# Another order of loads and other slots for the K and V tiles of a cached attention block

## The chip, the cores and the metric

The kernel runs on one core of one Trainium2 chip. The metric is the device time of one execution in microseconds. A core has five engines with an instruction list each: TensorE (PE: matmuls, PEld: its weight loads), VectorE (DVE), ScalarE (ACT), GpSimd (POOL) and SyncE (SP), which here only issues loads and stores. Each engine works through its list in order; engines wait for each other on semaphores. Sixteen DMA engines, shared by all loads, move data from the chip's memory (HBM) into the on-chip memory (SBUF).

## The reference, cut to what matters

One decode step: two batch rows `x` of 512 numbers go through a layer norm, an attention over a cache of 32768 keys and values in 8 key/value heads (32 query heads, 128 numbers each), and a gated two-layer network whose result scales the attention's output. All is float32.

```python
xn = layernorm(x)                                   # x: (2, 1, 512)
q = (xn @ wq) -> (2, 32, 1, 128)                    # 4 query heads share one K/V head
scores = einsum("bhqd,bhkd->bhqk", q, k) * 128**-0.5   # k, v: (2, 8, 32768, 128)
s = einsum("bhqk,bhkd->bhqd", softmax(scores), v) -> (2, 1, 4096) @ wo
gate = xn @ W_gate; up = xn @ W_up
g = silu(((gate * (gate > 0)) * up) @ W_down)
out = x + s * g
```

The caches are 2 x 268 MB, read once; everything else is small.

## The kernel before

The 16 pairs of batch row and K/V head are the **groups** (`NG` = 16, index `g`). A group's K and its V are two tiles each, K0, K1, V0, V1, of 16384 keys: 128 partitions x 16384 numbers, 8 MB. Such a tile fills one of three large SBUF slots. The weights `wq` (a full slot), `W_gate` with `W_up` (a slot together), `W_down` and, at the end, `wo` use the same slots.

What is done in a group (`attend`): VectorE transposes K0 in place in blocks of 32 (`turn`, L487, one instruction) and K1 in two halves; TensorE forms the scores of both (`score`, 32 matmuls a tile, into the PSUM tile `s`). Then comes the softmax: VectorE takes the maximum (L509), a chain of short TensorE and VectorE steps makes the bias, ScalarE the exponentials (L532), TensorE permutes them (`pts`), VectorE transposes them into `pt` (L542) and makes the reciprocal of the sum (L555). TensorE multiplies them with V0 and V1 (`values`, 32 matmuls a tile, into `o_ps`), and `gather` scales the result (L578) and folds it into `stage` (L599).

Ahead of the groups stands the **head**: the query projection from `wq`, whose result goes to `qz`; the products with `W_gate` and `W_up` (PSUM tile `pts`), three VectorE steps on them (L448, L452, L454), and the product with `W_down` (PSUM tile `m_ps`). Behind them stands the **tail**: `gather_all` puts the heads together (`ot_ps`, `ot`), and the product with `wo`, in six pieces (16, 8, 4, 2, 1 and 1 of its 32 rows a partition), ends in `res` and four small stores.

What sets the order. `Program.add` writes down, for each operation, which tiles it reads and writes, and derives its waits from that. Each engine's list is the order in which `add` is called; nothing reorders it. All loads but that of `x` are issued by SP, so they too are one list: a load that waits for its slot holds up all loads behind it. Slots go round: load number n goes to slot n mod 3, and `freed(n)`, called behind the last use of load n, issues load n + 3. The order of the tiles is K0, K1, V0, V1 of a group, then the next group. TensorE's list for the first 15 groups is a hardware loop of 5 trips with three groups as its body (`emit_loop`), since after three groups (12 tiles) the slots repeat; the other engines' lists are written out.

GpSimd clears and fills small constant tiles at the start (L246 to L281, L329) and copies the queries of each group into one of three buffers `qg` (L612).

Of the kernel before, what the change touches and what calls it, by code (L numbers as in the profile page):

```python
# [3 lines left out]
F32 = mybir.dt.float32  # L4
# [6 lines left out]
Q = 32  # L11
# [119 lines left out]
def decode_block(nc, x, kc, vc, wq, wo, wg, wu, wd, out):  # L131
# [19 lines left out]
    def sb(name, *shape):  # L151
        return nc.alloc_sbuf_tensor(name, list(shape), F32).ap()

    ring = [nc.alloc_sbuf_tensor(f"r{k}", [P, SLOT], F32, align_bytes=512).ap() for k in range(SLOTS)]
# [4 lines left out]
    qz = sb("qz", P, NG, 4, CR)  # L159
    qg = [sb(f"qg{k}", P, CR + P) for k in range(SLOTS)]  # L160
    place = sb("place", P, 3 + CR + 1)
    eye = sb("eye", P, 2 * P - CR)
    same = sb("same", P, Q, REP)
# [23 lines left out]
    def G(emit, reads=(), writes=()):  # L187
        pr.add("pool", emit, reads, writes)
# [19 lines left out]

    def freed(n):
        n += SLOTS  # L210
        g, i = divmod(n - SLOTS, 4)
        dst, names = slot(n)
        if g == NG and i == 0:
            worows = wo.rearrange("(p i) d -> p (i d)", p=P)
            row = 0
            for k, m in enumerate(WO_PIECES):
                span = slice(row * D, (row + m) * D)
                load(dst[:, span], worows[:, span], f"wo{k}", [("wo", k)] + (names if k == 0 else []))
                row += m
        elif g < NG:  # L220
            rows, kind = rows_of((kc, vc)[i // 2], g, i % 2), "kkvv"[i] + str(i % 2)
            if g == NG - 1 and i == 3:
                m = SLOT // 2
                for s in range(NS):
                    part = slice(s * m, (s + 1) * m)
                    load(dst[:, part], rows[:, part], kind + "b" * s, names[s : s + 1])
            else:
                load(dst, rows, kind, names)


    wqs, gus, wds = ring[:3]
    load(wqs[:, : NKC * QN], wq.rearrange("(p i) n -> p (i n)", p=P), "wq", slot(0)[1])
    for n, (src, kind) in enumerate(((wg, "wg"), (wu, "wu"))):
        load(
            gus[:, n * NKC * F : (n + 1) * NKC * F],
            src.rearrange("(p i) f -> p (i f)", p=P),
            kind,
            [(1, n)],
        )
    load(wds[:, : FI * D], wd.rearrange("(p i) d -> p (i d)", p=P), "wd", slot(2)[1])  # L240
    xp, xc = pt[:32, 0], pt[:32, 1]
# [83 lines left out]
    )  # L325
    n = 1
    while n < Q:
        G(
            lambda n=n: pool.tensor_copy(same[:, n : 2 * n, :], same[:, :n, :]),  # L329
            ["same"],  # L330
            ["same"],
        )
        n *= 2
    V(
# [42 lines left out]
        ),  # L377
        ["xnp"] + slot(0)[1],
        ["S"],
    )  # L380
    freed(0)
    V(lambda: dve.tensor_copy(w, S), ["S"], ["w"])  # L382
# [45 lines left out]
    for n in range(2):  # L428
        T(
            lambda n=n: matmuls(  # L430
                (
                    pts[32 * c : 32 * c + 32, n, :FC],
                    xnp[:, i, :],
                    gut[:, n, i, c * FC : (c + 1) * FC],
                    i == 0,
                    i == NKC - 1,
                )
                for i in range(NKC)
                for c in range(4)
            ),  # L440
            ["xnp", (1, n)],
            ["pts"],
        )
    freed(1)
    gate = w[:, 0, :FC]
# [11 lines left out]
    )  # L457
    T(
        lambda: matmuls(
            (  # L460
                m_ps[32 * (i % 4) : 32 * (i % 4) + 32, :],
                ht[:, i, :],
                wdt[:, i, :],
                i < 4,
                i >= FI - 4,
            )
            for i in range(FI)
        ),
        ["pt0"] + slot(2)[1],
        ["m"],  # L470
    )
    freed(2)
    part_d = os.rearrange("p c d -> p (c d)")
    V(lambda: dve.tensor_copy(part_d, m_ps), ["m"], OS)
    T(
        lambda: matmuls(
            (ot_ps[32 * c : 32 * c + 32, :P], fold, part_d[:, c * P : (c + 1) * P], True, True)
            for c in range(4)
        ),
        ["fold"] + OS,  # L480
        ["ot_ps"],
    )
    A(lambda: act.activation(gy, ot_ps[:, :P], AF.Silu), ["ot_ps"], ["gy"])


    def turn(tile, names, part):
        V(lambda: dve.transpose(tile[:, part], tile[:, part]), names, names)  # L487

    def score(g, u, s, tile, names):
        mov = tile.rearrange("p (s c j e k) -> p s c e j k", s=NS, c=NC, j=NJ, e=4)  # L490
# [12 lines left out]
            ),  # L503
            [f"qg{g % SLOTS}", names[s]],
            ["S"],
        )

    def softmax(g):
        V(lambda: dve.tensor_reduce(mx, S, axis=AX.XY, op=ALU.max), ["S"], ["mx"])  # L509
        T(lambda: pe.transpose(m_ps[:1, :P], mx, ident), ["mx", "ident"], ["m"])  # L510
        V(
            lambda: dve.tensor_reduce(  # L512
# [43 lines left out]

    def values(g, u, ss, tile, names):
        v = tile.rearrange("p (s c j d) -> p s j c d", s=NS, c=NC, j=NJ)
# [15 lines left out]

    def gather(g):
        b, hk = g % B, g // B
        V(
# [31 lines left out]
    def queries(g):  # L609
        k = g % SLOTS  # L610
        to = qg[k][:, CR:].rearrange("p (e q) -> p e q", e=4)[:, :, :CR]
        G(lambda: pool.tensor_copy(to, qz[:, g]), QZ, [f"qg{k}"])  # L612

    whole, half = slice(0, SLOT), SLOT // 2

    def attend(g):
        last = g == NG - 1
        queries(g)
        first = SLOTS + 4 * g
        k0, k1, v0, v1 = (slot(first + i) for i in range(4))  # L620
        turn(*k0, whole)
        for s in range(NS):
            turn(k1[0], k1[1][s : s + 1], slice(s * half, (s + 1) * half))
        for u, k in enumerate((k0, k1)):
            for s in range(NS):
                score(g, u, s, *k)
            freed(first + u)
        softmax(g)
        values(g, 0, range(NS), *v0)
        freed(first + 2)  # L630
        if last:
            for s in range(NS):
                values(g, 1, [s], *v1)
        else:
            values(g, 1, range(NS), *v1)
        freed(first + 3)
        gather(g)

    pr.add("pe", None, ["same", "place", "ident", "negs", "pt1"] + PERM, ["S", "pts", "m", "r", "o"])
    start = len(pr.ops["pe"])  # L640
    for g in range(NG):
        attend(g)
        if g == NG - 2:
            end = len(pr.ops["pe"])


    def gather_all(hks):
        return matmuls(
            (
                ot_ps[:, : B * Q],  # L650
                eye[:CR, P - CR - CR * hk : 2 * P - CR - CR * hk],
                stage[:CR, hk].rearrange("p b i -> p (b i)"),
                hk == 0,
                hk == HKV - 1,
            )
            for hk in hks
        )
# [10 lines left out]
    )  # L668
    wos, _ = slot(SLOTS + 4 * NG)
# [5 lines left out]
    py, pw = S[:, 0], S[:, 1]  # L675
    V(lambda: dve.memset(pw, 0.0), writes=["S", "pw"])  # L676
    bounds = [sum(WO_PIECES[:k]) for k in range(len(WO_PIECES) + 1)]
# [98 lines left out]
```

## Time and profile before

| | |
|---|---|
| time, median of 3 runs (lowest, highest) | 1314.77 us (1313.4, 1315.34) |
| the profiled execution: its time, its span | 1313.29 us, 1311.4 us |
| PE busy | 665.6 us (51%), 4680 matmuls |
| DVE busy | 632.2 us (48%), 204 instructions |
| ACT, POOL busy | 23.7 us (2%), 8.7 us (1%) |
| mean granted TensorE clock | 0.748 of full speed |
| read from HBM | 564.66 MB, 431 GB/s over the span |

The span runs from the first to the last instruction of the profiled execution, and its times count from the span's start. A row of the timeline gives start, duration, engine, line and operation, then in brackets how long the engine had been idle and what released it; "x64" counts merged instructions, and a float32 matmul of the program appears as two passes. L202 is the line of a helper that issues nearly all matmuls, so matmuls are told apart by their tiles: `s<-r,qg` are scores, `o_ps<-r,pt` are values.

### The profile page before, as it was taken

Reading aid. Unit: us, or ns where it says so; the run is one execution under the profiler, and the core shown is the slowest. Engines: PE = TensorE matmul, PEld = TensorE weight load, DVE = VectorE, ACT = ScalarE, POOL = GpSimd, SP = SyncE. Lnnn points to the kernel's source line nnn. Section 1 sums busy time; section 2 is a strip of 40 time slices with the busy share of each in tenths; the row PEclk is TensorE's granted clock in tenths of the full one; section 3 lists DMA queues with packets and bytes.
Section 4 is the critical chain, followed back from the end, with each engine's and each line's share of the span. In section 5 each row is a group of like instructions: output and inputs, shape, how many; then the busy total and the mean of one; then the engine's idle time right before and its main releaser. Section 6 shows DMA issues by size and latency. Waiting matters only on the chain.

```text
span 1311.4 us, 9865 instructions
## 1 busy us (share of the span) xinstructions
PE 665.6 (51%) x4680; PEld 186.2 (14%) x4680; DVE 632.2 (48%) x204; ACT 23.7 (2%) x37; POOL 8.7 (1%) x43
## 2 busy tenths in 40 slices
PE   3536164472616538262563726356372645637268
PEld 0202011120101102010110201011020111201012
DVE  1183562817356191744719165370925527183560
ACT  0000000000000000000000000000000000000000
POOL 1000000000000000000000000000000000000000
PEclk9768687785868777586776758778676877867688
DMA  9999999999999999999999999999999999999997
GB/s 409 438 444 422 440 424 436 428 434 442 432 434 434 432 432 434 442 434 432 434 432 436 436 438 434 430 434 434 442 428 438 434 430 434 432 444 430 436 424 331
DMA packets 10834, 564.88 MB, mean 431 GB/s; under 512 B 1210, under 2 KB 1218, under 8 KB 1604
## 3 DMA queue, kind: packets, MB, share of 16 engines
q1 hardware_dynamic: 10808, 564.67, 99.5%
q8 instruction: 11, 0.18, 0.0%
q14 instruction: 3, 0.02, 0.0%
q10 hardware_dynamic: 12, 0.01, 0.0%
HBM read 564.66 MB, written 0.00 MB: 431 GB/s over the span
## 4 chain that ended last, share of the span: by engine, by line
DMA 47%; DVE 26%; PE 25%; ACT 1%; issue 1%; DVEq 0%
DMA r<-in_A_k_cache_dram 45%; DVE r L487 21%; PE o_ps L202 11%; PE s L202 8%; PE pts L202 5%; DMA r<-in_A_wq_dram 2%; DVE pt L542 2%; DVE mx L509 2%; ACT w L532 1%; PE m_ps L202 1%; DVE mr L512 0%; PE m_ps L510 0%; DVE mrow L519 0%; DVE nb L530 0%; PE ot_ps L202 0%
## 5 line engine op out<-in xcount | busy, mean ns | idle before, releaser
L487 DVE STREAM_TRANSPOSE r<-r 128x8192 f32<-128x8192 f32 (+1 forms) x48 | 552.8, 11542 | 171.1 <-DMA r<-in_A_k_cache_dram 171.1
L202 PE MATMUL s<-r,qg 128*32 128x512 f32 x2048 | 296.4, 737 | 523.3 <-DVE r L487 523.3
L202 PE MATMUL o_ps<-r,pt 128*16 128x512 f32 x2048 | 247.6, 645 | 18.8 <-DVE rl L555 18.0
L202 PEld LDWEIGHTS s<-r,qg 128*32 128x32 f32 x2048 | 71.0, 132 | 738.1 <-DVE r L487 556.8
L578 DVE SCALAR_TENSOR_TENSOR os<-o_ps,rl,mask 128x512 f32<-128x512 f32 x16 | 12.0, 751 | 251.2 <-PE o_ps L202 251.2
L202 PEld LDWEIGHTS o_ps<-r,pt 128*16 128x16 f32 x2048 | 57.6, 103 | 195.5 <-issue 173.4
L509 DVE TENSOR_REDUCE mx<-s 128x1 f32<-128x1024 f32 x16 | 19.6, 1225 | 92.7 <-PE s L202 92.7
L202 PE MATMUL pts<-w,perm 128*128 128x512 f32 x64 | 51.9, 958 | 23.8 <-ACT w L532 23.8
L542 DVE STREAM_TRANSPOSE pt<-pts 128x1024 f32<-128x1024 f32 x16 | 20.0, 1250 | 73.2 <-PE pts L202 73.2
L532 ACT ACTIVATE w<-s,nb 128x1024 f32<-128x1024 f32 x16 | 17.8, 1113 | 1197.3 <-DVE nb L530 1197.3
L202 PE MATMUL r_ps<-os,place 128*16 128x128 f32 x128 | 16.8, 274 | 15.6 <-DVE os L578 15.6
L202 PEld LDWEIGHTS pts<-w,perm 128*128 128x128 f32 x64 | 15.0, 258 | 37.4 <-ACT w L532 25.2
L202 PEld LDWEIGHTS r_ps<-os,place 128*16 128x16 f32 x128 | 11.1, 96 | 31.5 <-DVE os L578 30.3
L510 PE MATMUL m_ps<-ident,mx 128*1 128x128 f32 x16 | 4.3, 270 | 21.7 <-DVE mx L509 21.7
L202 PE MATMUL s<-r,xnp 128*32 128x512 f32 x64 | 8.7, 706 | 9.1 <-DMA r<-in_A_wq_dram 9.1
L599 DVE TENSOR_REDUCE stage<-r_ps 16x32 f32<-16x128 f32 x16 | 4.5, 278 | 18.2 <-PE r_ps L202 18.2
L202 PEld LDWEIGHTS m_ps<-l,same 128*128 128x128 f32 x32 | 10.8, 337 | 16.0 <-issue 16.0
L202 PE MATMUL m_ps<-negs,mrow 1*128 1x1 f32 x32 | 6.6, 272 | 9.9 <-DVE mrow L519 9.9
L612 POOL COPY qg<-qz 128x64 f32<-128x64 f32 x16 | 3.7, 236 | 1019.3 <-PE s L202 996.9
L202 PE MATMUL pts<-r,xnp 128*32 128x448 f32 x64 | 8.8, 716 | 1.9 <-DVE qz L417 1.9
L202 PE MATMUL s<-r,ot 128*2 128x512 f32 (+1 forms) x88 | 8.8, 553 | 0.9 <-DVE s L676 0.9
L382 DVE COPY w<-s 128x1024 f32<-128x1024 f32 x1 | 1.2, 1225 | 16.5 <-PE s L202 16.5
(71 smaller groups left out, 77.1 us busy)
## 6 DMA issues: line engine op xcount, KB each, us to landing
r<-in_A_v_cache_dram SPq DMA_DIRECT2D x2, 4096.0 KB, 28.5
r<-in_A_wo_dram SPq DMA_DIRECT2D x1, 4096.0 KB, 26.7
r<-in_B_W_gate_dram SPq DMA_DIRECT2D x1, 3584.0 KB, 29.8
r<-in_B_W_up_dram SPq DMA_DIRECT2D x1, 3584.0 KB, 39.3
r<-in_B_W_down_dram SPq DMA_DIRECT2D x1, 3584.0 KB, 47.1
r<-in_A_wo_dram SPq DMA_DIRECT2D x1, 2048.0 KB, 31.2
r<-in_A_wo_dram SPq DMA_DIRECT2D x1, 1024.0 KB, 33.1
r<-in_A_k_cache_dram SPq DMA_DIRECT2D x32, 35.5
```

Of the source, the lines that this page charges most:

```text
L202: ins = pe.matmul(out_, lhs, rhs, start=start, stop=stop)
L382: V(lambda: dve.tensor_copy(w, S), ["S"], ["w"])
L487: V(lambda: dve.transpose(tile[:, part], tile[:, part]), names, names)
L509: V(lambda: dve.tensor_reduce(mx, S, axis=AX.XY, op=ALU.max), ["S"], ["mx"])
L510: T(lambda: pe.transpose(m_ps[:1, :P], mx, ident), ["mx", "ident"], ["m"])
L532: lambda: act.activation(w, S, AF.Exp, bias=nb, scale=SCALE, accum_out=l),
L542: lambda: dve.transpose(pt.rearrange("p u n -> p (u n)"), pts.rearrange("p u n -> p (u n)")),
L578: lambda: dve.scalar_tensor_tensor(os, o_ps, rl, mask.unsqueeze(2).to_broadcast([P, NC, DH]), op0=ALU.mult, op1=ALU.mult,),
L599: lambda: dve.tensor_reduce(stage[:CR, hk, b], r_ps[:CR, :P].rearrange("p (c i) -> p i c", c=NC), axis=AX.X, op=ALU.add,),
L612: G(lambda: pool.tensor_copy(to, qz[:, g]), QZ, [f"qg{k}"])
```

## The change

The three slots get fixed tenants: `SB` the K0 tiles, `SA` the K1 tiles, `SC` the V0 and V1 tiles in turn. K runs one group ahead: while a group's values are formed, the K tiles of the next group are loaded and scored. The order of loads is therefore K, V, K, V: V1 of g, K0 of g + 2, V0 of g + 1, K1 of g + 2. `wq` stands in `SA`, `W_gate` with `W_up` and then `W_down` in `SC`, and K0 of group 0 is loaded as the second tile, into `SB`. A trip of `attend(g)` is now: scores of K0 of g + 1, values of V0 of g, scores of K1 of g + 1, values of V1 of g, softmax of g + 1 (`weights`) with the scaling and gathering of g inside it. TensorE's loop has one group as its body and 15 trips; the scores of group 0 stand ahead of the loop, the values of group 15 behind it. Most of `gather_all` (7 of 8 heads) comes ahead of the values of the last V1. The four constant tiles `qz`, `qg`, `place`, `eye` are cut from one tile `zero` that one instruction clears, `qg` is one buffer in place of three, and `same` is filled by one copy with a repeated operand in place of five.

```diff
+    SA, SB, SC = (...)                       # three slots, not a ring
+    load(wqs, wq, "wq", SA[1])
+    load_tile(SB, 0, 0, 0)                   # K0 of group 0
     W_gate, W_up -> SC
-    load(wds[:, : FI * D], wd..., "wd", slot(2)[1])
...
     query projection from SA
+    load_tile(SA, 0, 0, 1)                   # K1 of group 0
     products with W_gate, W_up
+    load(wds[:, : FI * D], wd..., "wd", SC[1])
     gate, gate * up, transpose into pt        # VectorE
+    queries(0)
+    scores(0)                                # K0 of group 0
+    load_tile(SB, 0, 1, 0)                   # K0 of group 1
     product with W_down
+    load_tile(SC, 1, 0, 0)                   # V0 of group 0
     part_d copy, fold, silu
+    scores(1)                                # K1 of group 0
+    load_tile(SA, 0, 1, 1)                   # K1 of group 1
+    queries(1)
+    maximum()
+    weights()
...
+    def scores(u):
+        tile, names = (SB, SA)[u]
+        if u == 0:
+            turn(tile, names, whole)
+        for s in range(NS):
+            if u == 1:
+                turn(tile, names[s : s + 1], slice(s * half, (s + 1) * half))
+        for s in range(NS):
+            score(u, s, tile, names)
     def attend(g):
+        ahead, last = g + 2, g == NG - 2
+        scores(0)
+        values(0, range(NS), *SC)
+        load_tile(SC, 1, g, 1)
+        if last:
+            load_tile(SB, 1, g + 1, 0)
+        else:
+            load_tile(SB, 0, ahead, 0)
+        scores(1)
+        if not last:
+            queries(ahead)
+        maximum()
+        values(1, range(NS), *SC)
+        if last:
+            load_tile(SA, 1, g + 1, 1, NS)
+        else:
+            load_tile(SC, 1, g + 1, 0)
+            load_tile(SA, 0, ahead, 1)
+        weights(g)
...
+    values(0, range(NS), *SB)
+    gather_all(range(HKV - 1))
+    for s in range(NS):
+        values(1, [s], *SA)
+    take()
+    gather(NG - 1)
+    gather_all(range(HKV - 1, HKV))
...
-    pr.emit_loop("pe", ops[start:end], (NG - 1) // SLOTS)
+    pr.emit_loop("pe", ops[start:end], NG - 1)
```

Three places show what moved. The first is the start of SP's list of loads; `r0`, `r1`, `r2` are the three slots before, `ra`, `rb`, `rc` are `SA`, `SB`, `SC`. Before:

```order
L195 DMA r0<-in_A_wq_dram 128x16384 [waits barrier_Pool_Activation_PE_DVE_SP_release]
L195 DMA r1<-in_B_W_gate_dram 128x7168
L195 DMA r1<-in_B_W_up_dram 128x7168
L195 DMA r2<-in_B_W_down_dram 128x7168
L195 DMA r0<-in_A_k_cache_dram 128x16384 [waits pe]
L195 DMA r1<-in_A_k_cache_dram 128x16384 [waits pe]
L195 DMA r2<-in_A_v_cache_dram 128x16384 [waits pe]
L195 DMA r0<-in_A_v_cache_dram 128x16384 [waits pe]
```

And now:

```order
L198 DMA ra<-in_A_wq_dram 128x16384 [waits barrier_Pool_Activation_PE_DVE_SP_release]
L198 DMA rb<-in_A_k_cache_dram 128x16384
L198 DMA rc<-in_B_W_gate_dram 128x7168
L198 DMA rc<-in_B_W_up_dram 128x7168
L198 DMA ra<-in_A_k_cache_dram 128x16384 [waits pe]
L198 DMA rc<-in_B_W_down_dram 128x7168 [waits pe]
L198 DMA rb<-in_A_k_cache_dram 128x16384 [waits pe]
L198 DMA rc<-in_A_v_cache_dram 128x16384 [waits pe]
L198 DMA ra<-in_A_k_cache_dram 128x16384 [waits pe]
L198 DMA rc<-in_A_v_cache_dram 128x16384 [waits pe]
L198 DMA rb<-in_A_k_cache_dram 128x16384
```

`W_down` is now sixth in the list, behind both K tiles of group 0, and waits for TensorE; the second load into `rb` is K0 of group 1, the first loads of V0 and V1 into `rc` follow with K1 of group 1 between them.

The second place is VectorE's list from the gate's three steps up to the first maximum. Before:

```order
L448 TENSOR_SCALAR w<-pts 128x448 [waits pe]
L452 TENSOR_TENSOR w<-w,pts 128x448 [waits dve]
L454 STREAM_TRANSPOSE pt<-w 128x448 [waits dve]
L474 COPY os<-m_ps 128x512 [waits pe]
L487 STREAM_TRANSPOSE r<-r 128x16384 [waits k0]
L487 STREAM_TRANSPOSE r<-r 128x8192 [waits k1]
```

And now:

```order
L431 TENSOR_SCALAR w<-pts 128x448 [waits pe]
L435 TENSOR_TENSOR w<-w,pts 128x448 [waits dve]
L437 STREAM_TRANSPOSE pt<-w 128x448 [waits dve]
L443 STREAM_TRANSPOSE rb<-rb 128x16384 [waits k0]
L629 COPY os<-m_ps 128x512 [waits pe]
L443 STREAM_TRANSPOSE ra<-ra 128x8192 [waits k1]
```

The transpose of K0 has moved ahead of the copy of the `W_down` product, which now stands between the transposes of K0 and K1.

The third place is TensorE's loop body as it is now, up to the softmax; the queries (`qg`) are read from the tile `zero`.

```order
L202 MATMUL s<-rb,zero 32x512 [waits pool,dve]
L202 MATMUL s<-rb,zero 32x512 x31
L202 MATMUL o_ps<-rc,pt 16x512 [waits v0]
L202 MATMUL o_ps<-rc,pt 16x512 x31
L202 MATMUL s<-ra,zero 32x512 [waits dve]
L202 MATMUL s<-ra,zero 32x512 x15
L202 MATMUL o_ps<-rc,pt 16x512 [waits v1]
L202 MATMUL o_ps<-rc,pt 16x512 x31
L468 MATMUL m_ps<-ident,mx 1x128 [waits dve]
```

Scores and values alternate, where before a group had its 64 score matmuls, its softmax, and then its 64 value matmuls; the second half of K1's scores, which reads like the first, is left out of the rows.

More of the change, by code (lines that the diff above doesn't have):

```diff
@@ L152, in sb @@
         return nc.alloc_sbuf_tensor(name, list(shape), F32).ap()
-    ring = [nc.alloc_sbuf_tensor(f"r{k}", [P, SLOT], F32, align_bytes=512).ap() for k in range(SLOTS)]
+    SA, SB, SC = (
+        (nc.alloc_sbuf_tensor(f"r{k}", [P, SLOT], F32, align_bytes=512).ap(), [(k, 0), (k, 1)])
+        for k in "abc"
+    )
     ident, xy, gy, res, perm, fold = (
@@ L158, in decode_block @@
     )
[L159 to L162, printed above, removed]
+    sizes = (NG * 4 * CR, CR + P, 3 + CR + 1, 2 * P - CR)
+    zero = sb("zero", P, sum(sizes))
+    ends = [sum(sizes[:k]) for k in range(len(sizes) + 1)]
+    qz, qg, place, eye = (zero[:, a:b] for a, b in zip(ends, ends[1:]))
+    qz = qz.rearrange("p (g e c) -> p g e c", g=NG, e=4)
     same = sb("same", P, Q, REP)
@@ L207, in rows_of, with load_tile @@
         return src[b, hk, u * TK : (u + 1) * TK, :].rearrange("(p r) d -> p (r d)", p=P)
[L209 to L232, printed above, removed]
+    def load_tile(where, kv, g, u, parts=1):
+        dst, names = where
+        rows, kind = rows_of((kc, vc)[kv], g, u), "kv"[kv] + str(u)
+        m = SLOT // parts
+        for s in range(parts):
+            part = slice(s * m, (s + 1) * m)
+            tag = f"{kind}_{s}" if parts > 1 else kind
+            load(dst[:, part], rows[:, part], tag, names if parts == 1 else names[s : s + 1])
+    wqs, gus, wds = SA[0], SC[0], SC[0]
+    load(wqs[:, : NKC * QN], wq.rearrange("(p i) n -> p (i n)", p=P), "wq", SA[1])
+    load_tile(SB, 0, 0, 0)
     for n, (src, kind) in enumerate(((wg, "wg"), (wu, "wu"))):
@@ L237, in decode_block @@
             kind,
-            [(1, n)],
+            SC[1][n : n + 1],
         )
-    load(wds[:, : FI * D], wd.rearrange("(p i) d -> p (i d)", p=P), "wd", slot(2)[1])
     xp, xc = pt[:32, 0], pt[:32, 1]
@@ L325, in decode_block @@
     )
[L326 to L333, printed above, removed]
+    G(
+        lambda: pool.tensor_copy(
+            same[:, 1:, :], same[:, :1, :].to_broadcast([P, Q - 1, REP])
+        ),
+        ["same"],
+        ["same"],
+    )
     V(
@@ L377, in decode_block @@
         ),
-        ["xnp"] + slot(0)[1],
+        ["xnp"] + SA[1],
         ["S"],
     )
-    freed(0)
+    load_tile(SA, 0, 0, 1)
     V(lambda: dve.tensor_copy(w, S), ["S"], ["w"])
@@ L440, in decode_block @@
             ),
-            ["xnp", (1, n)],
+            ["xnp", SC[1][n]],
             ["pts"],
         )
-    freed(1)
+    load(wds[:, : FI * D], wd.rearrange("(p i) d -> p (i d)", p=P), "wd", SC[1])
     gate = w[:, 0, :FC]
@@ L457, in decode_block, with score @@
     )
[L458 to L483, printed above, removed]
     def turn(tile, names, part):
         V(lambda: dve.transpose(tile[:, part], tile[:, part]), names, names)
-    def score(g, u, s, tile, names):
+    def score(u, s, tile, names):
         mov = tile.rearrange("p (s c j e k) -> p s c e j k", s=NS, c=NC, j=NJ, e=4)
@@ L503, in score, with maximum, weights @@
             ),
-            [f"qg{g % SLOTS}", names[s]],
+            ["qg", names[s]],
             ["S"],
         )
-    def softmax(g):
+    def maximum():
         V(lambda: dve.tensor_reduce(mx, S, axis=AX.XY, op=ALU.max), ["S"], ["mx"])
+    def weights(done=None):
         T(lambda: pe.transpose(m_ps[:1, :P], mx, ident), ["mx", "ident"], ["m"])
+        if done is not None:
+            take()
         V(
@@ L535, in softmax @@
         )
+        if done is not None:
+            gather(done)
         T(
@@ L555, in softmax, with values @@
         V(lambda: dve.reciprocal(rl, m_ps[:, 300:301]), ["m"], ["rl"])
-    def values(g, u, ss, tile, names):
+    def values(u, ss, tile, names):
         v = tile.rearrange("p (s c j d) -> p s j c d", s=NS, c=NC, j=NJ)
@@ L573, in values, with take @@
         )
-    def gather(g):
-        b, hk = g % B, g // B
+    def take():
         V(
@@ L609, in queries @@
     def queries(g):
-        k = g % SLOTS
-        to = qg[k][:, CR:].rearrange("p (e q) -> p e q", e=4)[:, :, :CR]
-        G(lambda: pool.tensor_copy(to, qz[:, g]), QZ, [f"qg{k}"])
+        to = qg[:, CR:].rearrange("p (e q) -> p e q", e=4)[:, :, :CR]
+        G(lambda: pool.tensor_copy(to, qz[:, g]), QZ, ["qg"])
     whole, half = slice(0, SLOT), SLOT // 2
-    def attend(g):
[L617 to L630, printed above, removed]
+    def scores(u):
[7 more added lines that the diff above has]
+            score(u, s, tile, names)
@@ L631, in attend @@
+    def attend(g):
+        ahead, last = g + 2, g == NG - 2
+        scores(0)
+        values(0, range(NS), *SC)
+        load_tile(SC, 1, g, 1)
         if last:
-            for s in range(NS):
-                values(g, 1, [s], *v1)
-        else:
[L635 to L644, printed above, removed]
@@ new lines, in attend @@
+        scores(1)
[12 more added lines that the diff above has]
+    load_tile(SB, 0, 1, 0)
+    T(
+        lambda: matmuls(
+            (
+                m_ps[32 * (i % 4) : 32 * (i % 4) + 32, :],
+                ht[:, i, :],
+                wdt[:, i, :],
+                i < 4,
+                i >= FI - 4,
+            )
+            for i in range(FI)
+        ),
+        ["pt0"] + SC[1],
+        ["m"],
+    )
@@ L662, in decode_block @@
+    load_tile(SC, 1, 0, 0)
+    part_d = os.rearrange("p c d -> p (c d)")
+    V(lambda: dve.tensor_copy(part_d, m_ps), ["m"], OS)
+    T(
+        lambda: matmuls(
+            (ot_ps[32 * c : 32 * c + 32, :P], fold, part_d[:, c * P : (c + 1) * P], True, True)
+            for c in range(4)
+        ),
+        ["fold"] + OS,
         ["ot_ps"],
     )
+    A(lambda: act.activation(gy, ot_ps[:, :P], AF.Silu), ["ot_ps"], ["gy"])
+    scores(1)
+    load_tile(SA, 0, 1, 1)
+    queries(1)
+    maximum()
@@ new lines, in decode_block @@
+    weights()
+    pr.add(
+        "pe", None, ["same", "place", "ident", "negs", "pt0", "pt1"] + PERM, ["S", "pts", "m", "r", "o"]
+    )
+    start = len(pr.ops["pe"])
+    for g in range(NG - 1):
+        attend(g)
+    end = len(pr.ops["pe"])
+    wos = SC[0]
+    worows = wo.rearrange("(p i) d -> p (i d)", p=P)
+    row = 0
+    for k, m in enumerate(WO_PIECES):
+        span = slice(row * D, (row + m) * D)
+        load(wos[:, span], worows[:, span], f"wo{k}", [("wo", k)] + (SC[1] if k == 0 else []))
+        row += m
@@ new lines, in decode_block, with gather_all @@
+    py, pw = S[:, 0], S[:, 1]
+    V(lambda: dve.memset(pw, 0.0), writes=["S", "pw"])
+    def gather_all(hks):
+        T(
+            lambda: matmuls(
+                (
+                    ot_ps[:, : B * Q],
+                    eye[:CR, P - CR - CR * hk : 2 * P - CR - CR * hk],
+                    stage[:CR, hk].rearrange("p b i -> p (b i)"),
+                    hk == 0,
+                    hk == HKV - 1,
+                )
+                for hk in hks
+            ),
+            ["eye"] + [("stage", g) for hk in hks for g in range(hk * B, hk * B + B)],
+            ["ot_ps"],
+        )
@@ L664, in decode_block @@
+    values(0, range(NS), *SB)
+    gather_all(range(HKV - 1))
+    for s in range(NS):
+        values(1, [s], *SA)
+    take()
+    gather(NG - 1)
+    gather_all(range(HKV - 1, HKV))
     V(
```

27 lines of the change are left out of this document (4 added, 23 removed).

## The prediction

> **What bounds the kernel now.** I read the page's head first: the forty slices, the queues, the chain.
>
> ```profile
> span 1311.4 us, 9865 instructions
> DMA  9999999999999999999999999999999999999997
> GB/s 409 438 444 422 440 424 436 428 434 442 432 434 434 432 432 434 442 434 432 434 432 436 436 438 434 430 434 434 442 428 438 434 430 434 432 444 430 436 424 331
> q1 hardware_dynamic: 10808, 564.67, 99.5%
> DMA 47%; DVE 26%; PE 25%; ACT 1%; issue 1%; DVEq 0%
> ```
>
> The chain gives DMA only 47%, but it is misleading: the DMA engines are full in 39 of 40 slices at one rate. No engine can make the middle shorter; only a gap in the DMA stream can make it longer, and only the last slice has room to win. So the question is whether SP still issues each load before the queue runs dry. How early it does so now is in the list of DMA issues, and a load's own length in VectorE's timeline:
>
> ```profile
> r<-in_A_k_cache_dram SPq DMA_DIRECT2D x32, 35.5
> r<-in_A_v_cache_dram SPq DMA_DIRECT2D x31, 47.7
> r<-in_A_wq_dram SPq DMA_DIRECT2D x1, 21.8
> 1150.95 17.25 DVE L487 STREAM_TRANSPOSE r<-r 128x16384 f32<-128x16384 f32 x1 [7.32 <-DMA r<-in_A_k_cache_dram]
> 1228.14 17.25 DVE L487 STREAM_TRANSPOSE r<-r 128x16384 f32<-128x16384 f32 x1 [6.74 <-DMA r<-in_A_k_cache_dram]
> 1247.45 17.30 DVE L487 STREAM_TRANSPOSE r<-r 128x8192 f32<-128x8192 f32 x2 [2.06 <-DMA r<-in_A_k_cache_dram]
> ```
>
> The transposes start when K0 and K1 land: 1247.45 - 1228.14 = **19.3 us** a tile, and 1228.14 - 1150.95 = 77.2 us a group, four tiles. A K load lands 35.5 us after its issue, so it was issued 16 us before its turn; a V load 28 us. `wq`, the one load that met an empty queue, took 21.8 us: an empty queue costs 2.5 us more than a full one.
>
> **The change: the start.** Here the new order puts waits into SP's list that weren't there. Durations:
>
> ```profile
> 22.64 8.74 PE L202 MATMUL s<-r,xnp 128*32 128x512 f32 x64 [9.07 <-DMA r<-in_A_wq_dram]
> 37.97 8.75 PE L202 MATMUL pts<-r,xnp 128*32 128x448 f32 x64 [1.87 <-DVE qz L417]
> 46.80 0.62 DVE L448 TENSOR_SCALAR w<-pts 128x448 f32<-128x448 f32 x1 [8.88 <-PE pts L202]
> 48.11 0.94 DVE L454 STREAM_TRANSPOSE pt<-w 128x448 f32<-128x448 f32 x1
> 49.42 5.32 PE L202 MATMUL m_ps<-r,pt 128*32 128x512 f32 x28 [2.70 <-DMA r<-in_B_W_down_dram]
> 54.78 0.69 DVE L474 COPY os<-m_ps 128x512 f32<-128x512 f32 x1 [5.73 <-PE m_ps L202]
> 85.97 9.49 PE L202 MATMUL s<-r,qg 128*32 128x512 f32 x64 [30.02 <-DVE r L487]
> 163.23 8.42 PE L202 MATMUL s<-r,qg 128*32 128x512 f32 x64 [27.57 <-DVE r L487]
> 1245.44 10.02 PE L202 MATMUL s<-r,qg 128*32 128x512 f32 x64 [24.36 <-DVE r L487]
> ```
>
> `wq` lands at 22.6 and `W_down` at 49.4, so the three loads of 3584 KB take 26.8 us, 8.9 each (by size, 7/16 of 19.3, 8.4). In the new list K0 comes between: `W_up` lands at 22.6 + 19.3 + 2 x 8.9 = 59.7; call this moment U. Behind it the queue holds K1 of group 0 (issued at 31.4, when the query projection is done) and `W_down` (issued when the `W_up` product is done): it runs dry at U + 19.3 + 8.4 = U + 27.7. The next load in SP's list is K0 of group 1, into `SB`, which waits for the scores of K0 of group 0. That tile has lain there since 41.9, but its transpose stands in VectorE's list behind the three steps of the gate, and these wait for `W_up`. So the issue comes after: the `W_up` product (half of 8.75 us, but started after a pause, see below: 5.0; bounds 3.0 and 6.0), the gate's steps (46.80 to 49.05: 2.3), the transpose 17.3, the scores 9.5 (bounds 8.4 and 10.0), 0.1 of hand-overs. That is U + 34.2, and it lands 21.8 later, at U + 56.0; in an unbroken stream it would have been U + 47.0. **First gap: 9.0 us.** With a start from empty at only 19.3 it would be 6.5; I take the row of `wq`, the only such start.
>
> Call this issue T. What follows on the engines, with the softmax's rows:
>
> ```profile
> 105.33 4.93 PE L202 MATMUL s<-r,qg 128*32 128x512 f32 x32 [4.95 <-DVE r L487]
> 1187.61 6.50 PE L202 MATMUL s<-r,qg 128*32 128x512 f32 x32 [4.95 <-DVE r L487]
> 1194.18 1.22 DVE L509 TENSOR_REDUCE mx<-s 128x1 f32<-128x1024 f32 x1 [6.63 <-PE s L202]
> 119.10 7.06 PE L202 MATMUL o_ps<-r,pt 128*16 128x512 f32 x64 [1.12 <-DVE rl L555]
> 1203.20 0.13 DVE L555 RECIPROCAL rl<-m_ps 128x1 f32<-128x1 f32 x1
> 1264.81 5.34 PE L202 MATMUL s<-r,qg 128*32 128x512 f32 x32 [4.95 <-DVE r L487]
> 1270.21 1.23 DVE L509 TENSOR_REDUCE mx<-s 128x1 f32<-128x1024 f32 x1 [5.46 <-PE s L202]
> 1278.20 0.13 DVE L555 RECIPROCAL rl<-m_ps 128x1 f32<-128x1 f32 x1
> ```
>
> From T on: the `W_down` product right behind the scores (28 passes at the 0.11 us of a warm array, 7.06 / 64: 3.1; at most the 5.3 of its row), the copy of it 0.7, which VectorE's list puts ahead of K1's transpose, that transpose 17.3, the second half of the scores 5.6 (4.9 to 6.5), the maximum and the softmax 8.7 (1270.21 to 1278.33 is 8.1, 1194.18 to 1203.33 is 9.2). VectorE is free at T + 35.4. Only then does it transpose K0 of group 1, which landed at T + 21.8: 17.3, scores 9.5, values of V0 7.1, and V1 of group 0 can be issued at T + 69.3, to land at T + 91.1. Unbroken, K0, V0, K1 and V1 would have landed at T + 21.8 + 3 x 19.3 = T + 79.7. **Second gap: 11.4 us.** K1 of group 1 (issued at about T + 27) and V0 (T + 3) are in time.
>
> **The loop** then has less lead than before. V0 of the next group waits for the values of V1, V1 for those of V0, because both live in `SC`. From K0's landing to the issue of V1: 17.3 + 10.0 + 7.1 = 34.4 by the slowest rows. The queue then still holds V0 and K1, 38.6 us from that landing, less 2.5 for a start from empty: a margin of **1.7 us**, 3.3 by the fast row. Is VectorE free when K0 lands? K0 lands 19.3 after V1; K1, 19.3 before V1, needs 17.3 + 6.5, so its scores end 4.5 after V1's landing; values 7.1; softmax less its maximum 7.9, with the scaling (L578) now inside it about 0.8 more: 20.3, at worst 1.0 late. V0's own issue, at 11.6, has 19.3 - 2.5: no risk. So the loop stays full, at 77.2 us a group; cost nothing, the cover being the K1 load that is running. If the margin is gone, each of the 14 further trips pays the excess.
>
> **The tail** gains a little:
>
> ```profile
> r<-in_A_wo_dram SPq DMA_DIRECT2D x2, 256.0 KB, 34.1
> 1270.20 2.70 SPq L195 DMA_DIRECT2D r<-in_A_wo_dram  x6
> 1278.34 15.80 PE L202 MATMUL o_ps<-r,pt 128*16 128x512 f32 x128 [1.12 <-DVE rl L555]
> 1299.40 8.21 PE L202 MATMUL s<-r,ot 128*2 128x512 f32 x72 [0.91 <-DVE s L676]
> 1307.25 0.69 DVE L712 COPY w<-s 128x512 f32<-128x512 f32 x1 [7.90 <-PE s L202]
> 1308.21 0.62 PE L202 MATMUL s<-r,ot 128*2 128x128 f32 x16
> 1308.90 0.29 DVE L722 TENSOR_TENSOR res<-s,gy 128x128 f32<-128x128 f32 x1 [0.96 <-PE s L202]
> 1309.54 0.66 SPq L195 DMA_DIRECT2D out_dram<-res  x2
> ```
>
> The last piece of `wo`, issued near 1272.5, lands at 1306.6, but the `wo` matmuls start only at 1299.40, because the last group's softmax and 15.80 us of values stand before them; the stores go out 2.9 us after the last landing. Now the last scores and softmax are two loads earlier, the matmuls follow the pieces, and behind the last landing stand some 0.4 us of matmuls and 0.6 of VectorE: stores at +1.1. **Gain 1.8 us** (1 to 2.5).
>
> GpSimd's shorter list (8.7 us busy in all, on no part of the chain) and TensorE's ten more loop returns, which fall into the 24 to 30 us idle before K0's scores in the rows above, cost and bring nothing; with that cover gone a return could cost no more than the wait it sits in.
>
> Sum: 9.0 + 11.4 - 1.8 = **+18.6 us** on the profiled execution's own 1313.29: 1331.9. Its span of 1311.4 leaves 1.9 around it, which stays. The median is 1.5 above that execution; I forecast **1332**.
>
> A row on the array's clock: after an idle stretch the scores run 9.49 for 64 passes, warm they would be 64 x 0.11 = 7.0. The Trainium skill, "TensorE: Matmul & The Clock Gate", Part 1, states that the array falls to half clock after an idle window of about 3.4 us and needs as long to recover; the trace agrees, with 4.93 to 6.50 us for 32 passes after 4.95 idle against 3.5 warm. If it stayed warm, both gaps would be 2.5 shorter and the sum 13.6. On starts from empty, "DMA: Bandwidth & Descriptors", Anatomy of one DMA, in the Trainium skill, fits 2.0 us plus the bytes at 436 GB/s, estimated 21.2 for a tile, where the trace has 21.8; by it the first gap is 0.6 smaller, the second unchanged.
>
> **Rivals.** (1) *The loop runs dry too.* For it: 1.7 us of margin less up to 1.0 of lateness, where there were 16. Against: those are the slowest rows together, and a late trip delays V1 and thereby gives K1's scores more time. From an issue later than 36.1 us after K0's landing it decides; at 1.5 us a trip, 14 trips cost 21: **1353**. The Trainium skill speaks for this one: "DMA: Bandwidth & Descriptors", Rules for kernel authors, advises issuing early and waiting late so that the fixed cost overlaps; one slot for V0 and V1 does the reverse. No trace here shows a dry loop.
> (2) *No gap: K0 of group 0 is transposed when it lands*, at 41.9, not behind the gate. Then its scores end about U + 15, K0 of group 1 is issued well ahead of U + 25, and the second gap closes as well: the `W_down` product waits for its load at U + 27.7, VectorE is free at about U + 66, V1 is issued at U + 100, and the queue holds until U + 105. Only the tail's 1.8 is left: **1313**. It decides if VectorE's list lets the transpose pass the gate; the order rows speak against it.
> (3) *One gap only*: were K1 of group 0 transposed ahead of the copy of the `W_down` product, VectorE would be through with the first softmax at about T + 22, as K0 of group 1 lands, V1 would be issued at T + 56, and the second gap would vanish: 1313.29 + 9.0 - 1.8 = **1320.5**. The list's order is against it too.
>
> **The numbers.** Forecast 0.78, rival 1 0.14, rival 2 0.05, rival 3 0.03. The forecast's own bounds: all fast rows (product 3.0, scores 8.4 twice, start 19.3, softmax and scores short) take 8 off, all slow ones add 5.5, so 1324 to 1337.5. To hold 8 in 10, the range goes on into rival 1 with up to half a microsecond a trip: **1324 to 1345**. A change within 0.2%, about 2.6 us, is what a measurement cannot tell from none: faster 0.02, same 0.04, slower 0.94.
>
> **What would show it.** Right: the windows show DMA idle in two places, near 90 and near 155 to 165 us, and a full queue after; K0 of group 1 is issued near 94; SP's waits fall on `s` once and `o_ps` once there; the stores follow the last `wo` landing by about 1.1. Wrong: DMA shares under 1 in every group (rival 1), a K0 transpose that starts near 42 (rival 2), a tile time other than 19.3.

## The result, and the profile after

The changed kernel takes 1330.19 us (median of 4 runs, 1329.82 to 1331.33) against 1314.16 us of the kernel before: a ratio of 1.0123 with a 95% interval of 1.0105 to 1.014. It is slower by 16 us; the forecast was 1332. The profiled spans, 1328.1 and 1311.4 us, differ by 16.7, where the forecast's sum was 18.6. Of the page of the changed kernel, the slices and the chain:

```profile
span 1328.1 us, 9811 instructions
DMA  9979799999999999999999999999999999999998
GB/s 411 441 334 411 317 441 424 431 440 440 420 436 440 440 416 440 440 440 414 442 438 438 418 440 440 428 428 438 434 436 428 438 434 434 430 436 434 434 425 356
DMA 57%; DVE 24%; PE 16%; another core or an unknown queue 2%; SPq 0%; issue 0%; ACT 0%
```

Before, only the last slice moved fewer than 400 GB/s. Now the third and the fifth do too, 334 and 317, a slice being 33 us long: two holes, both before 170 us, and none behind them. The chain's shares (DMA 57% in place of 47%, PE 16% in place of 25%) do not show the holes. The holes closer up, from the windows of the changed kernel (columns: window, its length, busy time of PE, PEld, DVE, ACT and POOL with instruction counts, granted clock, DMA share, GB/s):

```profile
88.00:90.00 2.00, 2.00 (x24) 0.60 (x20) 0.00 (x0) 0.00 (x0) 0.00 (x0) 1.00 0.04 8
90.00:92.00 2.00, 2.00 (x24) 0.54 (x20) 0.00 (x0) 0.00 (x0) 0.00 (x0) 1.00 0.00 0
154.00:156.00 2.00, 2.00 (x26) 0.46 (x20) 1.06 (x1) 0.00 (x0) 0.00 (x0) 1.00 0.00 0
158.00:160.00 2.00, 2.00 (x24) 0.44 (x16) 2.00 (x1) 0.00 (x0) 0.00 (x0) 1.00 0.00 0
```

No load is under way, and TensorE works without a pause: its work is what the next load waits for. The timelines of SP, TensorE and VectorE name it:

```profile
59.98 4.66 PE L202 MATMUL pts<-rc,xnp 128*32 128x448 f32 x32 [3.47 <-DMA rc<-in_B_W_up_dram]
66.91 17.20 DVE L443 STREAM_TRANSPOSE rb<-rb 128x16384 f32<-128x16384 f32 x1
84.16 8.38 PE L202 MATMUL s<-rb,zero 128*32 128x512 f32 x64 [19.51 <-DVE rb L443]
92.61 0.33 SPq L198 DMA_DIRECT2D rb<-in_A_k_cache_dram  x1
96.02 0.69 DVE L629 COPY os<-m_ps 128x512 f32<-128x512 f32 x1 [11.91 <-PE m_ps L202]
127.52 17.22 DVE L443 STREAM_TRANSPOSE rb<-rb 128x16384 f32<-128x16384 f32 x1
144.79 8.78 PE L202 MATMUL s<-rb,zero 128*32 128x512 f32 x64 [18.32 <-DVE rb L443]
153.40 7.04 PE L202 MATMUL o_ps<-rc,pt 128*16 128x512 f32 x64
154.94 17.31 DVE L443 STREAM_TRANSPOSE ra<-ra 128x8192 f32<-128x8192 f32 x2 [10.20 <-DMA ra<-in_A_k_cache_dram]
160.51 0.33 SPq L198 DMA_DIRECT2D rc<-in_A_v_cache_dram  x1
203.19 17.25 DVE L443 STREAM_TRANSPOSE rb<-rb 128x16384 f32<-128x16384 f32 x1 [5.48 <-DMA rb<-in_A_k_cache_dram]
```

K0 of group 0 has been in its slot since about 42 us; its transpose starts at 66.91, right behind the gate's steps, its scores end at 92.5, and SP issues K0 of group 1 at 92.61. The second stretch is the same story one round later: VectorE comes free at 127.5, transposes K0 of group 1, TensorE scores it and forms the values of V0, and V1 of group 0 is issued at 160.51, 5.6 us after K1 landed (154.94) and left the queue empty.

The sizes follow from the list of DMA issues of the changed kernel, over the stretch around each issue, in the order `W_down`, K0 of group 1, V0 of group 0, V1 of group 0 (the last number is the time from issue to landing):

```profile
rc<-in_B_W_down_dram SPq DMA_DIRECT2D x1, 3584.0 KB, 23.0
rb<-in_A_k_cache_dram SPq DMA_DIRECT2D x1, 21.8
rc<-in_A_v_cache_dram SPq DMA_DIRECT2D x1, 39.6
rc<-in_A_v_cache_dram SPq DMA_DIRECT2D x1, 22.0
```

`W_down`, issued at 64.7, landed at 87.7; K0 of group 1 landed at 92.6 + 21.8 = 114.4, which is 26.7 us later, where a load in a full queue takes 19.3: the first gap is **7.4 us**. V0, issued at 96.0, landed at 135.6, 21.2 after K0: 1.9 us more are lost in a queue that was not empty. V1 landed at 160.5 + 22.0 = 182.5, 27.6 after K1: the second gap is **8.3 us**. K0 of group 2 landed at 203.2, 20.7 after V1: 1.4 us more. Together 19.0 us; less the 1.7 us that the tail gains (below) that is 17.3, against the 16.7 between the spans. Of the 0.6 left over, 0.5 stands in the head: `W_up` landed 9.5 us behind `W_gate`, and 10.0 us in the kernel before.

The loop costs nothing. The transposes of K0 of groups 2 and 15 stand at 203.19 (above) and 1207.91 in the changed kernel, and at 223.45 and 1228.14 (in the prediction) in the kernel before:

```profile
223.45 17.25 DVE L487 STREAM_TRANSPOSE r<-r 128x16384 f32<-128x16384 f32 x1 [9.21 <-DMA r<-in_A_k_cache_dram]
1207.91 17.25 DVE L443 STREAM_TRANSPOSE rb<-rb 128x16384 f32<-128x16384 f32 x1 [2.92 <-DMA rb<-in_A_k_cache_dram]
```

In both, 13 groups take 1004.7 us, 77.3 each. VectorE waited 2.5 to 5.5 us for each of these K0 tiles. At the tail of the changed kernel, the last matmuls, the last VectorE step and the stores stand thus:

```profile
1324.75 0.76 PE L202 MATMUL s<-rc,ot 128*2 128x128 f32 x16
1325.90 0.29 DVE L744 TENSOR_TENSOR res<-res,xy 128x128 f32<-128x128 f32 x1
1326.22 0.66 SPq L198 DMA_DIRECT2D out_dram<-res  x2
rc<-in_A_wo_dram SPq DMA_DIRECT2D x2, 256.0 KB, 46.5
```

The six pieces of `wo` were issued from 1276.2 to 1278.5, so the last landed near 1325.0, and the stores went out 1.2 us later, where it was 2.9 before.

### The profile page after: what moved, and what is told of

It is laid out like the page before. It is cut to its first block, busy times and chain, and to the rows that moved or that the text cites. A ratio compares the mean times of both kernels' runs of the same rounds, so it can differ in the third digit from the quotient of the medians.

```text
span 1328.1 us, 9811 instructions
## 1 busy us (share of the span) xinstructions
PE 636.8 (48%) x4680; PEld 179.3 (14%) x4680; DVE 630.4 (47%) x204; ACT 23.7 (2%) x37; POOL 7.7 (1%) x34
## 4 chain that ended last, share of the span: by engine, by line
DMA 57%; DVE 24%; PE 16%; another core or an unknown queue 2%; SPq 0%; issue 0%; ACT 0%
DMA ra<-in_A_k_cache_dram 47%; DVE ra L443 20%; PE o_ps L202 8%; PE s L202 7%; DVE rb L443 4%; DMA rc<-in_B_W_gate_dram 4%; DMA rc<-in_A_wo_dram 3%; DMA rb<-in_A_k_cache_dram 3%; PE pts L202 1%; SPq L198 0%; PE m_ps L202 0%; PE m_ps L468 0%; DVE pt L504 0%; DVE mx L465 0%
## 5 line engine op out<-in xcount | busy, mean ns | idle before, releaser
L443 DVE STREAM_TRANSPOSE ra<-ra 128x8192 f32<-128x8192 f32 x32 | 276.9, 8690 | 309.8 <-DMA ra<-in_A_k_cache_dram 309.8
L202 PE MATMUL s<-rb,zero 128*32 128x512 f32 x1024 | 147.4, 740 | 345.3 <-DVE rb L443 345.3
L443 DVE STREAM_TRANSPOSE rb<-rb 128x16384 f32<-128x16384 f32 x16 | 275.8, 17240 | 48.2 <-DMA rb<-in_A_k_cache_dram 48.2
L202 PE MATMUL s<-ra,zero 128*32 128x512 f32 x1024 | 165.7, 807 | 254.5 <-DVE ra L443 254.5
L202 PE MATMUL o_ps<-rc,pt 128*16 128x512 f32 x1920 | 212.9, 596 | 5.0 <-DMA rc<-in_A_v_cache_dram 5.0
L202 PEld LDWEIGHTS s<-rb,zero 128*32 128x32 f32 x1024 | 35.7, 133 | 444.6 <-DVE rb L443 347.4
L202 PEld LDWEIGHTS s<-ra,zero 128*32 128x32 f32 x1024 | 38.1, 142 | 381.1 <-DVE ra L443 283.5
L202 PEld LDWEIGHTS o_ps<-rc,pt 128*16 128x16 f32 x1920 | 53.3, 97 | 159.7 <-issue 153.8
L202 PE MATMUL pts<-w,perm 128*128 128x512 f32 x64 | 32.6, 633 | 9.2 <-ACT w L492 9.2
L202 PE MATMUL r_ps<-os,zero 128*16 128x128 f32 x128 | 16.8, 274 | 1.0 <-DVE os L539 1.0
L202 PE MATMUL m_ps<-negs,mrow 1*128 1x1 f32 x32 | 6.0, 256 | 17.3 <-DVE mrow L479 17.3
```

The source lines that it names most:

```text
L202: ins = pe.matmul(out_, lhs, rhs, start=start, stop=stop)
```

## The experiments

The theory (A): the loss is two dry stretches of the load queue in the first 165 us, each made by one engine's order; the loop costs nothing; the tail gains some 1.6 us. The rival (B): the loop pays for its late V1 loads, and the start is not what counts. Twelve kernels were run, each beside the kernel before on the same chip.

### The first gap: K0 of group 0 transposed when it lands

```diff
     QZ = ["qz"] + [("qz", kb) for kb in range(4)]
+    turn(*SB, slice(0, SLOT))
     gut = gus[...]                            # products with W_gate, W_up, the gate
...
-    scores(0)
+    scores(0, False)                          # without the transpose
```

> The changed kernel with one move: VectorE transposes K0 of group 0 ahead of the three steps of the gate, so when it lands (near 42 us). Theory A (the loss is two dry stretches of the load queue at the start, each set by one engine's order): the first gap goes (7.4 us and the 1.9 us lost right behind it), but the second grows, since the W_down product now starts only when its load lands: VectorE through with the first softmax at about 124.5, V1 of group 0 issued near 157.6 and landed near 179.4, where an unbroken queue would have it at 164.8: gap 14.6. Time 1327 to 1330. As rival 2 of the prediction was written (both gaps go): 1313. Theory B (the loop's short lead costs, the start does not): 1330.

1327.12 us, ratio 1.0098 (1.0081 to 1.0115). Rival 2's price of 1313 falls, A's corrected sum, 1327 to 1330, holds. SP's and VectorE's timelines of this kernel:

```profile
71.94 0.33 SPq L198 DMA_DIRECT2D rb<-in_A_k_cache_dram  x1
93.78 17.29 DVE L410 STREAM_TRANSPOSE ra<-ra 128x8192 f32<-128x8192 f32 x2
146.09 17.30 DVE L410 STREAM_TRANSPOSE ra<-ra 128x8192 f32<-128x8192 f32 x2 [4.22 <-DMA ra<-in_A_k_cache_dram]
157.67 0.33 SPq L198 DMA_DIRECT2D rc<-in_A_v_cache_dram  x1
```

K0 of group 1 is issued at 71.94, 16 us before the queue's end: no first gap. But the `W_down` product now waits for its load (88 us), K1's transpose still waits for the copy of that product (93.78), and V1 is issued at 157.67, 11.6 us after K1 of group 1 landed at 146.09. One gap was closed, and the other took most of it back.

### The second gap: K1 of group 0 transposed ahead of the copy

```diff
     load_tile(SB, 0, 1, 0)
+    for s in range(NS):
+        turn(SA[0], SA[1][s : s + 1], slice(s * half, (s + 1) * half))
     T(...)                                    # product with W_down, then its copy
...
-    scores(1)
+    scores(1, False)
```

> The changed kernel with another single move: both halves of K1 of group 0 are transposed ahead of the copy of the W_down product. Theory A: the first gap stays at 7.4 us, VectorE is through with the first softmax near 121 in place of 127.6, V1 of group 0 lands near 175.6 against 174.1 unbroken: the second gap shrinks from 8.3 to about 1.5. Time 1322 to 1325. As rival 3 of the prediction was written: 1320.5. Theory B: 1330.

1323.06 us, ratio 1.0069 (1.0052 to 1.0086), inside A's 1322 to 1325. V1 of group 0 was issued at 154.34, where it had been 160.51, as this kernel's SP timeline shows:

```profile
154.34 0.33 SPq L198 DMA_DIRECT2D rc<-in_A_v_cache_dram  x1
```

### Both, and the copy behind the scores

```diff
     (both edits above)
     scores(1, False)
     load_tile(SA, 0, 1, 1)
     queries(1)
     maximum()
+    part_d copy, fold, silu                   # stood ahead of scores(1)
     weights()
```

> Both moves, and the copy and fold of the W_down product put behind the scores of K1 and the maximum. Theory A: K0 of group 1 issued near 73, V1 of group 0 issued near 142 with the queue full until 145.5: at most 1 us of gap. Only the tail's gain is left: 1311 to 1314, that is the kernel before less about 1.6. Theory B: 1328 to 1330.

1313.57 us (10 runs), ratio 0.9995 (0.9986 to 1.0005): the loss against the kernel before is gone, and with it theory B, since the loop is the changed kernel's, instruction for instruction. A small gap is left, as the SP timeline and the list of DMA issues of this kernel show:

```profile
144.21 0.33 SPq L198 DMA_DIRECT2D rc<-in_A_v_cache_dram  x1
rc<-in_A_v_cache_dram SPq DMA_DIRECT2D x1, 22.4
```

V1 landed 22.4 us after its issue, as from an empty queue, though it was issued some 2 us before the queue's end.

### TensorE's loop with three groups as its body

```diff
-    pr.emit_loop("pe", ops[start:end], NG - 1)
+    pr.emit_loop("pe", ops[start:end], (NG - 1) // 3)
```

> The changed kernel with TensorE's loop as 5 trips of three groups in place of 15 trips of one; the order of all work is the same. Theory A: loop returns fall into TensorE's idle time before K0's scores: within 1.5 us of 1330. If the loop's returns cost time (rival): 10 returns fewer, at 0.5 us or more each, 1325 or less.

1330.36 us, ratio 1.0129 (1.0112 to 1.0146), as the changed kernel. The loop's returns cost nothing that can be measured.

### GpSimd's list alone, in the kernel before

```diff
-    qz = sb(...); qg = [sb(...) for k in range(SLOTS)]; place = sb(...); eye = sb(...)
+    zero = sb("zero", P, sum(sizes)); qz, qg, place, eye = (zero[:, a:b] ...)
-    six memsets, five copies into same
+    one memset of zero, one copy with a repeated operand
```

> The kernel before with the changes of GpSimd's list alone (one cleared tile, one buffer of queries, one copy with a repeated operand). Both theories: no part of it lies on the chain: 1313 to 1316, as before.

1314.35 us, ratio 1.0 (0.9991 to 1.0009). This part of the change does nothing to the time.

### How short the lead of a load may be

Extra matmuls on TensorE, in each trip, between K0's scores and V0's values, push the issue of V1 back:

```diff
         scores(0)
+        T(lambda: matmuls((r_ps[:, P : 2 * P], ident, ident, True, True) for _ in range(8)), ["ident"], ["r2"])
         values(0, range(NS), *SC)
```

> The changed kernel with 8 extra matmuls (128x128, into an unused part of a PSUM bank) on TensorE between K0's scores and V0's values in each trip: about 2.1 us more before each issue of V1. In the profile of the changed kernel V1 is issued 4.7 to 6.5 us before the queue runs out, and a start from empty costs 2.5. Theory A (the loop has some 2 us in hand and costs nothing): only the second gap grows, by 2.1: 1331 to 1334. Theory B (the loop pays for each late issue): 15 times 2.1, 1355 or more.

> The same with 24 extra matmuls, about 6.3 us. Theory A: the lead is gone; each of 14 trips pays 6.3 + 2.5 less a mean lead of 5.3, so 3.5, and the second gap 6.3: 1365 to 1395, with DMA idle in every group. If the loop had far more in hand than the profile shows: 1336.

> The changed kernel with 4 extra matmuls, 1.0 us, between K0's scores and V0's values in each trip. With 8 the leads fell to 2.8 to 3.5 us and a V1 load took 0.65 us longer in the mean; with none they are 4.3 to 6.5 and it takes no longer. Theory A2 (a load must be issued some 3.5 us ahead of the queue's end, more than the 2.5 of a single start): leads of 3.4 to 5.5, only the shortest pay: 1331 to 1335. If each microsecond of delay costs whatever the lead is: half of what 8 matmuls added, 1338.

Measured: 4 extra matmuls 1339.42 us (four runs, 1334.37 to 1343.46; ratio 1.0194, 1.0165 to 1.0223), 8 of them 1346.29 (ratio 1.0245, 1.0229 to 1.0261), 24 of them 1380.25 (2 runs). The long delay came out as A had it, the two short ones did not: 1346.29 is 12 us above A's range, and 4 matmuls cost 9 us where A2 had 1 to 5. The start takes part of it, the loop the rest: with 8 matmuls the span is 16.3 us longer than the changed kernel's, 5.0 of it up to the landing of K0 of group 2 and 11.3 in the trips behind. One trip each, from the timelines of SP and VectorE, first the changed kernel, then 8, then 24 extra matmuls (K1's landing is where its transpose starts):

```profile
623.60 0.33 SPq L198 DMA_DIRECT2D rc<-in_A_v_cache_dram  x1
628.06 17.30 DVE L443 STREAM_TRANSPOSE ra<-ra 128x8192 f32<-128x8192 f32 x2 [21.35 <-DMA ra<-in_A_k_cache_dram]
```

```profile
635.28 0.33 SPq L198 DMA_DIRECT2D rc<-in_A_v_cache_dram  x1
638.09 17.30 DVE L443 STREAM_TRANSPOSE ra<-ra 128x8192 f32<-128x8192 f32 x2 [21.70 <-DMA ra<-in_A_k_cache_dram]
679.17 17.25 DVE L443 STREAM_TRANSPOSE rb<-rb 128x16384 f32<-128x16384 f32 x1 [5.02 <-DMA rb<-in_A_k_cache_dram]
```

```profile
649.13 17.30 DVE L443 STREAM_TRANSPOSE ra<-ra 128x8192 f32<-128x8192 f32 x2 [21.35 <-DMA ra<-in_A_k_cache_dram]
650.00 0.33 SPq L198 DMA_DIRECT2D rc<-in_A_v_cache_dram  x1
```

The changed kernel's V1 has 4.5 us of lead over the queue's end here, and over all trips 4.4 to 5.9; none of the loads in its loop took longer than 19.3 us by more than 0.1. With 8 matmuls (2.05 us by the trace) the lead is 2.8, and V1 and K0 behind it land 41.1 us after K1, not 38.6: 2.5 us lost. That did not happen in each trip: the leads were 2.5 to 4.1, and the V1 loads took between 0 and 2.4 us longer, 0.6 in the mean of 14. With 24 the leads are -1.1 to 0.3, and each V1 load pays 2.0 to 3.7 us. So the need is nearer to 4 us than to the 2.5 that a start from empty costs, and between 2.5 and 4.1 the loss is irregular. (The expectations above put the leads at other figures, 4.7 or 4.3 to 6.5 without extra matmuls and 2.8 to 3.5 with 8; these are the leads by the rows.) That irregularity fits the wide range of the runs with 4 matmuls, whose leads were 3.3 to 4.8. Why 3 us of lead do not always do was not settled.

### Values ahead of scores

```diff
         ahead, last = g + 2, g == NG - 2
-        scores(0)
         values(0, range(NS), *SC)
         load_tile(SC, 1, g, 1)
+        scores(0)
```

> The changed kernel with two steps of a trip exchanged: the values of V0 (and the load of V1 that they set free) come ahead of the scores of the next K0. Theory A: V1 of group 0 is issued near 144 us, 10 us ahead of the queue's end, so the second gap (8.3 us) and the 1.4 us behind it go; in the loop the lead of V1's load grows from about 5 to about 10 us and brings nothing, since nothing was lost there: 1319 to 1322.5. Theory B (the short leads of the loop cost something too): below 1318.

> The kernel with the values first and the same 8 extra matmuls between the two halves of V0's values. Theory A2: the lead is still about 8 us, so the 2.1 us cost nothing: within 1.5 us of the kernel with the values first. If the extra matmuls themselves slow the loads or the loop: 10 us or more above it.

> That exchange and the early transpose of K0 of group 0 together. Theory A: neither gap is left, only the tail's gain: 1311 to 1313.5, as the kernel with the head of before (1311.65).

The exchange alone: 1320.57 us, ratio 1.0053 (1.0037 to 1.0068), as A had it. V1 of group 0 is issued at 143.98, 11 us before K1 lands:

```profile
143.98 0.33 SPq L198 DMA_DIRECT2D rc<-in_A_v_cache_dram  x1
```

The second gap is gone, the first is left. With 8 extra matmuls between the halves of V0's values it is 1320.51: the same 2.05 us of work that cost 16 us at a lead of 5 costs nothing where the lead is 9 to 11 and stays at 7 or more. So it was the lead that paid, not the extra work. The exchange together with the early transpose of K0 gives 1310.56 us, ratio 0.9975 (0.9963 to 0.9986), the lowest median of the study, though its interval overlaps that of the kernel with the old head (0.9971 to 0.9989, next). Of its page and its SP timeline:

```profile
span 1308.7 us, 9828 instructions
DMA  9999999999999999999999999999999999999998
136.78 0.33 SPq L198 DMA_DIRECT2D rc<-in_A_v_cache_dram  x1
1306.80 0.65 SPq L198 DMA_DIRECT2D out_dram<-res  x2
```

V1 of group 0 is issued 24 us earlier than in the changed kernel, and no slice but the last is short of full. Its span is 2.7 us shorter than the kernel before's: 1.7 by the tail, and 1.1 in one load, V0 of the last group, which took 20.4 us in the kernel before and 19.3 here.

### The head of the kernel before with the new loop

```diff
-    wqs, gus, wds = SA[0], SC[0], SC[0]
+    wqs, gus, wds = SB[0], SA[0], SC[0]       # K0, K1, V0 of group 0 follow them there
...
     scores(0), scores(1), weights()           # group 0
+    values(0, range(NS), *SC)                 # the first trip written out, V0's values first
...
-    for g in range(NG - 1):
+    for g in range(1, NG - 1):
```

> The changed kernel with the head of the kernel before: W_gate, W_up and W_down are loaded ahead of the K tiles of group 0, and the first trip is written out so that the values of V0 of group 0 come right after its softmax. Theory A: each of the first loads is issued at least 10 us ahead of its turn, no gap, the tail as in the changed kernel: 1311 to 1313.5, ratio to before about 0.9985. Theory B: no better than 1325.

1311.65 us (11 runs), ratio 0.998 (0.9971 to 0.9989). The new order of loads in the loop, with the old start, is a little faster than the kernel before, by the tail.

## Why the prediction was right, point by point

**What bounds the kernel** held: a tile takes 19.3 us in every kernel whose queue is full, and only gaps and the tail moved the time.

**The first gap**, forecast 9.0, was 7.4. The chain of steps was the forecast's; `W_up` landed just under 60 us, as worked out, and K0 of group 1 landed 21.8 us after its issue, the price taken from `wq`. The prediction's other price, an estimate of 21.2 us, goes by a fit that the Trainium skill, "DMA: Bandwidth & Descriptors", Anatomy of one DMA, gives for DMAs issued by GpSimd. The loads here are issued by SP, and from an empty queue no tile took less than 21.6 us. The gate's product and steps took about what was put down; the term with the largest error is the scores, 8.38 us by their row against 9.5, at the fast bound, so that the issue came at 92.6 and not at 93.9.

**The second gap**, forecast 11.4, was 8.3, but 1.9 us of it had been spent already, in the load of V0 ahead of it, which made K1 land later. The steps from T to the end of the first softmax came to 127.5 - 92.6 = 34.9 us against 35.4, and from there to the issue to 33.0 against 33.9; scores at 8.78 in place of 9.5 make most of that.

**What was not foreseen** are the 1.9 and 1.4 us behind the two gaps, in loads that were issued in good time. They made up for part of what the gaps fell short: 19.0 in all against 20.4. To that extent the closeness of the total is luck.

**The loop** was forecast at no cost with a margin of 1.7 us, and it cost nothing. The margin was reckoned with the wrong price: the lead was forecast as 38.6 - 34.4 = 4.2 at the slowest and was 4.4 to 5.9, but the point at which rival 1 begins is not a lead of 2.5 us, as the forecast put it, but one of about 4. The loop of the changed kernel stands just clear of it, so that the forecast of no cost was in part luck; one microsecond more of TensorE work in a trip already cost 9 us.

**The tail**, forecast 1.8, gained 2.9 - 1.2 = 1.7.

**Rival 2 was priced wrongly.** It said that with K0 transposed at once the second gap would close too, because V1 would be issued at U + 100 and the queue would hold until U + 105. But U + 105 is when V1 itself would have landed in an unbroken stream; the queue ends with K1, one load earlier, at U + 85.6. The first experiment is that rival carried out, and it took 1327.1, not 1313. It had been given 5% and did not touch the forecast, whose own gaps compare landing with landing.

**Rival 3** was about right in kind: the one move shrinks the second gap, to 1323.06 where 1320.5 was forecast. VectorE was through with the first softmax 28.5 us after the issue of K0 of group 1 (93.0 to 121.5), not 22, since the copy and fold of the `W_down` product still stood ahead of K1's scores.

## What to carry to other kernels

In a kernel whose loads never stop, a new order is judged by one question for each load: when is it issued, and when does the load ahead of it land? The steady state can pass that test while the start fails it, because at the start the engines' lists still hold steps of another stage, and an instruction that is ready waits behind one that is not. Here two moved lines, VectorE's transpose ahead of the gate and TensorE's values ahead of the scores, turned a loss of 16 us into a gain of 2 to 5; and a lead of 5 us per load should be read as just enough, not as plenty.

## What the runs showed of the hardware that was not expected

- **A load needs some 4 us of lead.** One that meets an empty queue takes 21.6 to 22.0 us for a tile in place of 19.3. But a lead of 2.5 to 4.1 us does not always spare that: in the kernel with 8 extra matmuls, V1 loads with such leads took up to 2.4 us longer. From 4.2 us on no V1 load of a loop took more than 19.4 us, in any of the kernels.
- **Behind a dry queue, a load with a packet of instructions among its data takes longer.** The load of V0 after the first gap and that of K0 after the second took 21.2 and 20.7 us although each was issued well ahead. The list of queues of the changed kernel, over 115 to 135 us, has one packet of instructions among the data,

```profile
q8 instruction: 1, 0.02, 0.3%
```

and so has the stretch from 183 to 203 us, while 137 to 154 and 205 to 222, whose loads took 19.3, have none. That the queue had been dry is not enough: in the kernel with 24 extra matmuls 13 loads of K0 stand behind a V1 that met an empty or nearly empty queue, and 12 of them, without such a packet, took 19.3 to 19.4 us. The other one took 20.3, and only the list over its stretch, 1153 to 1173 us, has a packet:

```profile
q14 instruction: 1, 0.01, 0.1%
```

Nor does every packet cost as much: behind a full queue many loads with one took 19.3 to 19.5 us, but V0 of the last group in the kernel before, with one at 1256.3, took 20.4. It may be that such a packet holds up one of the 16 engines, and that this counts only while the engines are level, as after a stop. That is an argument from where the packets stand; no run took one away, and the V0 of the kernel before had no stop shortly ahead of it. The irregular loss at leads of 2.5 to 4.1 us is something else: no V1 load with such a lead that took over 20 us has a packet among its data.
